# A kernel of attention and two feed-forward layers: elementwise work moved off GpSimd, plain products for 1,536 tokens, stored split weights, loads issued earlier

## Chip, cores, metric

One core of a Trainium2 chip. The metric is the device time of one execution in microseconds. The program is one kernel, written with an order of its own for every engine (no scheduler reorders it).

## What is computed

```python
scores = scale * np.matmul(q, k.transpose(0, 1, 3, 2))       # 4 x 8 heads, 576 tokens, 64
thresh = np.max(scores, axis=-1, keepdims=True) - tau
scores = np.where(scores >= thresh, scores, -1000000000.0)
attn = np.exp(scores - np.max(scores, axis=-1, keepdims=True))
attn = attn / (np.sum(attn, axis=-1, keepdims=True) + 1e-09)
x = np.matmul(attn, v)                                       # then 2304 tokens x 512
h = x @ w_in                                                 # layer one, 512 -> 2048
g = h * np.tanh(np.where(h > 20.0, h, np.log1p(np.exp(np.minimum(h, 20.0)))))
x = g @ w_out                                                # 2048 -> 512
y = ((x @ w_a) * (x @ w_b)) @ w_out2                         # layer two, 512 -> 1536 -> 512
```

q, k and v come as 32-bit floats, the weights as 64-bit floats.

## The kernel before

**Attention** runs in 80 units (16 pairs of heads, five units a pair), one per round of a loop. VectorE takes the scores from PSUM with their extreme (`least`) and masks the exponentials (`mask`), ScalarE forms the exponentials and copies transposed blocks out of PSUM, TensorE does scores, transposes and weighted sums. Results go to DRAM (`xd`).

**Conversion of weights.** `narrow` turns a 128-wide block of 64-bit weights into 32-bit ones by integer arithmetic on the two halves of each word, and writes it to DRAM (`wfd`). There are 68 such jobs. It is a generator: each `yield` is a place where it waits for its next turn. A job loads its raw block on SyncE's queue (`raw`), two turns later ScalarE and VectorE shift and mask it (lines 98 to 103), then GpSimd adds (107) and ScalarE squares (108), then VectorE masks small numbers to zero (110). In attention a job starts every `PACE` = 7 units; in the layers `narrow_some` gives each running job a turn per product.

**Layers.** Tokens are worked on in three superblocks of 768, each as two halves of 384. A step is a pair of 128-wide blocks of the hidden dimension: eight steps per superblock in layer one (h0 to h23), six in layer two (h24 to h41, each with products for w_a and for w_b). Every 32-bit operand is split into two parts (`hi` by ScalarE, the remainder by VectorE, line 155 for weights, 250 for x), and a product takes three matmuls for each of two 128-wide blocks. A step multiplies a 2 x 2 block matrix by seven products instead of eight: sums of blocks of the weights (`sums` in `in_weights`, tiles ws, GpSimd, line 181), sums of blocks of x (`sums` in `prepare`, GpSimd, 240), and combinations of the products afterwards (`after`: p1, p5 by ScalarE, u2, u3, c21, c12 by VectorE from PSUM, c22 by GpSimd, 342). Then the gate is applied (`gate` in layer one, the product of both branches in layer two), and `second` multiplies the result g by the out weights, one step later.

The place of a product is called a gap. `at_gap` hangs work into a later gap. Per gap the order of emission is: the product, what was hung there, a turn for conversions, some items of the weights of the next step (`feed`), the combination (`after`), the second products. Within an engine instructions run in this order. The weights' loads lead by two groups (one group is the weights of one kind for one step), in tiles `wf` with two buffers. The split weights of a step lie in one of three tiles (`wi_pools`). Products go to two PSUM tiles (`h`). `prepare` hangs the splits of x for a superblock into gaps from 6 before its start to 2 after it.

All loads and nearly all stores are issued from SyncE's queue, in order.

## Time and profile before

| | us |
|---|---|
| median of 3 runs | 1211.49 |
| lowest, highest | 1210.2, 1215.4 |
| the profiled execution | 1212.33 |
| its span, first to last instruction | 1210.5 |

| engine | busy us | share of the span |
|---|---|---|
| TensorE | 1116.2 | 92% |
| VectorE | 952.3 | 79% |
| ScalarE | 696.5 | 58% |
| GpSimd | 497.8 | 41% |

The engines are named PE, PEld (TensorE's weight loads), DVE (VectorE), ACT (ScalarE), POOL (GpSimd) and SP (SyncE). Matmuls are pipelined, so a busy TensorE is not one at its peak. An arrow names what was waited for. The share of busy time mixes stages with different limits: attention runs to about 295 us, layer one from there to 733, layer two to the end. The stretches below are cut at the first matmul of a step (h1 at 311.8, h8 at 447.7, h16 at 586.5, h24 at 733.5, h30 at 888.7, h36 at 1044.5).

### The profile page before, as it was taken

Reading aid. Unit: us, or ns where it says so; the run is one execution under the profiler, and the core shown is the slowest. Engines: PE = TensorE matmul, PEld = TensorE weight load, DVE = VectorE, ACT = ScalarE, POOL = GpSimd, SP = SyncE. Lnnn points to the kernel's source line nnn. Section 1 sums busy time; section 2 is a strip of 40 time slices with the busy share of each in tenths; the row PEclk is TensorE's granted clock in tenths of the full one; section 3 lists DMA queues with packets and bytes.
Section 4 is the critical chain, followed back from the end, with each engine's and each line's share of the span. In section 5 each row is a group of like instructions: output and inputs, shape, how many; then the busy total and the mean of one; then the engine's idle time right before and its main releaser. Section 6 shows DMA issues by size and latency. Waiting matters only on the chain.

```text
span 1210.5 us, 19202 instructions
## 1 busy us (share of the span) xinstructions
PE 1116.2 (92%) x6794; PEld 952.4 (79%) x6794; DVE 952.3 (79%) x1682; ACT 696.5 (58%) x1399; POOL 497.8 (41%) x502
## 2 busy tenths in 40 slices
...
GB/s 149 152 152 139 173 154 200 170 141 108 185 198 217 249 115 193 195 192 175 92 225 179 193 156 81 94 70 122 53 61 114 53 97 95 42 117 68 54 52 53
DMA packets 76993, 161.24 MB, mean 133 GB/s; under 512 B 6753, under 2 KB 36193, under 8 KB 76897
## 3 DMA queue, kind: packets, MB, share of 16 engines
...
q10 hardware_dynamic: 864, 1.08, 0.3%
...
## 4 chain that ended last, share of the span: by engine, by line
PE 60%; DVE 19%; issue 5%; DMA 5%; ACT 5%; POOL 4%; SPq 1%; DVEq 0%; POOLq 0%; ACTq 0%
PE acc L385 18%; PE tp L645 5%; PE sp L582 5%; PE sums_o L664 5%; DVE wii L155 2%; DVE wop L155 2%; DVE g L315 2%; DVE x L250 2%; DVE c21b L366 1%; POOL b L240 1%; DMA rawo<-w_out 1%; DVE s L590 1%; DVE woo L155 1%; DMA rawb<-w_b 1%; DVE pm L609 1%
## 5 line engine op out<-in xcount | busy, mean ns | idle before, releaser
L385 PE MATMUL acc<-g,woo 128*128 128x256 f32 (+1 forms) x1152 | 231.4, 344 | 0.0
L385 PEld LDWEIGHTS acc<-g,woo 128*128 128x128 f32 x1152 | 186.6, 194 | 17.4
L385 PE MATMUL acc<-g,wop 128*128 128x512 f32 (+1 forms) x864 | 172.2, 340 | 1.1 <-ACT g L320 0.7
L385 PEld LDWEIGHTS acc<-g,wop 128*128 128x128 f32 x864 | 139.0, 190 | 14.4 <-ACT g L320 0.9
L597 POOL TENSOR_TENSOR te<-m,bar 128x2 f32<-128x2 f32 (+1 forms) x80 | 44.8, 560 | 207.5 <-DVE s L590 207.5
L590 DVE TENSOR_SCALAR_CACHE_REDUCE s<-sp 128x576 f32<-128x576 f32 x144 | 103.4, 751 | 24.0 <-PE sp L582 20.4
L602 ACT ACTIVATE ex<-s,m 128x576 f32<-128x576 f32 x144 | 109.3, 771 | 16.1 <-DVE s L590 16.0
L646 ACT ACTIVATE pt<-tp 128x512 f32<-128x512 f32 (+1 forms) x192 | 90.8, 487 | 23.5 <-PE tp L645 21.6
L609 DVE SCALAR_TENSOR_TENSOR pm<-s,te,ex 128x576 f32<-128x576 f32 x128 | 100.7, 823 | 0.0
L645 PEld LDWEIGHTS tp<-ident,pm 128*128 128x128 f32 x576 | 63.4, 141 | 33.6 <-ACT ex L602 9.5
L645 PE MATMUL tp<-ident,pm 128*128 128x128 f32 x576 | 85.6, 280 | 4.5 <-ACT u L673 1.5
L315 DVE TENSOR_TENSOR g<-hs,g 128x384 fp32r<-128x384 f32 x96 | 84.8, 910 | 5.6 <-ACT g L314 5.4
L664 PE MATMUL sums_o<-pt,v 128*64 128x256 f32 x640 | 83.2, 390 | 0.0
L582 PE MATMUL sp<-k,qs 64*128 64x288 f32 x512 | 82.4, 429 | 0.8 <-DVE s L590 0.8
L342 POOL TENSOR_TENSOR c22a<-u3a,p5a 128x384 f32<-128x384 f32 x18 | 18.3, 1015 | 148.2 <-ACT p5a L340 148.2
L342 POOL TENSOR_TENSOR c22b<-u3b,p5b 128x384 f32<-128x384 f32 x18 | 19.7, 1094 | 125.0 <-DVE wop L155 91.8
L582 PEld LDWEIGHTS sp<-k,qs 64*128 64x128 f32 x512 | 46.5, 186 | 31.3 <-issue 8.6
L664 PEld LDWEIGHTS sums_o<-pt,v 128*64 128x64 f32 x640 | 40.3, 136 | 24.7 <-issue 7.1
L181 POOL TENSOR_TENSOR wsi<-wfi 128x256 f32<-128x256 f32 x48 | 50.0, 1041 | 19.4 <-DMA wfi<-wfi 19.4
L342 POOL TENSOR_TENSOR c22i<-u3i,p5i 128x384 f32<-128x384 f32 x24 | 29.2, 1219 | 55.0 <-ACT p5i L340 39.5
L155 DVE TENSOR_TENSOR wii<-wfi,wii 128x512 fp32r<-128x512 f32 (+1 forms) x48 | 45.4, 946 | 5.1 <-ACT wii L154 5.1
L155 DVE TENSOR_TENSOR woo<-wfo,woo 128x512 fp32r<-128x512 f32 x48 | 48.0, 1002 | 0.4
...
## 6 DMA issues: line engine op xcount, KB each, us to landing
...
```

Source lines behind the costliest of these rows:

```text
L155: lambda: V.tensor_tensor(out=dst()[1], in0=src(), in1=f32(dst()[0]), op=ALU.subtract),
L181: G.tensor_tensor(out=out, in0=x, in1=y, op=op)
L315: at_gap(gap + 1, lambda: V.tensor_tensor(out=gl, in0=hs, in1=f32(gh), op=ALU.subtract))
L342: G.tensor_tensor(out=o, in0=t["u3"], in1=t["p5"], op=ALU.add)
L385: PE.matmul(ps, w[:, a, f, c * 128:(c + 1) * 128], st.g[f][:, b, cols], start=st.first and f == 0 and m == 0 and (kind == "c" or c % 2 == ...
L582: PE.matmul(sp[:, half, 0:288], d["qs"][r, cols], d["k"][r, keys], start=True, stop=True)
L590: V.tensor_scalar(out=u["s"][:, h].rearrange("p (a c) -> p a c", a=2), in0=u["sp"][h][:, :, 0:288], scalar1=1.0, scalar2=None, op0=ALU.mul ...
L602: A.activation(u["e"][:, h], u["s"][:, h], AF.Exp, bias=u["m"][:, h:h + 1], scale=-1.0)
L609: V.scalar_tensor_tensor(out=u["pm"].rearrange("p a c -> p (a c)")[:, h * S:(h + 1) * S], in0=u["s"][:, h], scalar=u["te"][:, h:h + 1], in ...
L645: PE.transpose(tp[:, i], pm[:, j0 + i], ident)
L646: return lambda: A.activation(pt[:, j0:j0 + m], tp[:, :m], AF.Copy)
L664: PE.matmul(po[r], v[0][:, j + 4 * h, r], pair[pi][c & ~1][:, :, j + 4 * h], start=j == 0, stop=j == 4)
```

## The change

- The first two superblocks of layer one (`PLAIN`) are computed with eight plain products a step, two after one another into the same PSUM tile. Their weights are split as they are, without sums, x too (four splits instead of seven), and the gate reads PSUM directly.
- In the layers GpSimd gets no instruction any more: sums of weights and of x, c22 and the integer add of the conversion go to VectorE. In attention GpSimd keeps the add.
- A conversion has other instructions: one shift on VectorE instead of two masks, the mask for small numbers by a saturating copy on ScalarE and a clamp to -1 and 1 (by ScalarE in attention, by VectorE in the layers), then a product. The raw block is loaded four turns ahead instead of two. A job starts every 5 units in attention (16 jobs there instead of 12), and after that at rates of 0.45, 0.3, 0.3 per product and 0.25 in layer two.
- The split weights of w_a are stored in DRAM in the first superblock of layer two (from ScalarE's queue) and loaded as they are in the other two (1.8 MB a step, SyncE's queue).
- Loads of weights lead by three groups, in three buffers. A step of layer two has its w_a and out weights in its first seven gaps and w_b in the last seven.
- x of a superblock is made earlier, its sums in tiles of their own.

```diff
-T0, PACE = 1, 7
+T0, PACE = 1, 5
...
+PLAIN, PRE = {("i", 0), ("i", 1)}, {"i": 8, "a": 6}
+RATES = 0.45, 0.3, 0.3
...
-        yield A
-        yield A
-        u, a, o = tl("u", I32, 1), tl("a", I32, 2), tl("f", F32, 2)
-        A.activation(u, lo, AF.Copy, scale=2.0 ** -29)
-        V.tensor_scalar(
-            out=a, in0=hi.bitcast(I32), scalar1=3, scalar2=0x3FFFFFF8,
-            op0=ALU.logical_shift_left, op1=ALU.bitwise_and,
-        )
-        V.scalar_tensor_tensor(
-            out=a, in0=hi.bitcast(I32), scalar=-0x40000000, in1=a, op0=ALU.bitwise_and, op1=ALU.bitwise_or
+        for _ in range(4):
+            yield True
+        a, o = tl("a", I32, 2), tl("f", F32, 2)
+        A.activation(unit[:, 0::2].rearrange("p (c n) -> p c n", c=CC), lo, AF.Copy, scale=2.0 ** -29)
+        V.tensor_scalar(out=a, in0=hi.bitcast(I32), scalar1=3, scalar2=None, op0=ALU.logical_shift_left)
+        (G if acc_p is None else V).tensor_tensor(
+            out=a, in0=a, in1=unit.bitcast(I32).rearrange("p (c n) -> p c n", c=CC), op=ALU.add
...
-        yield G
-        G.tensor_tensor(out=a, in0=a, in1=u, op=ALU.add)
-        A.activation(o, hi.bitcast(F32), AF.Square)
-        yield V
-        V.scalar_tensor_tensor(out=o, in0=o, scalar=TINY, in1=a.bitcast(F32), op0=ALU.is_ge, op1=ALU.mult)
+        A.activation(o.bitcast(I32), hi.bitcast(F32), AF.Copy, scale=SEEN)
+        yield True
+        if acc_p is None:
+            A.activation(o, o.bitcast(I32), AF.Sign)
+        else:
+            V.tensor_scalar(out=o, in0=o.bitcast(I32), scalar1=-1.0, scalar2=1.0, op0=ALU.max, op1=ALU.min)
+        yield True
+        V.tensor_tensor(out=o, in0=a.bitcast(F32), in1=o, op=ALU.mult)
...
+    wpd = {
+        (kind, p): dram.tile([128, 2, 7, 256], F32, name=f"wp{kind}{p}") for kind, n in PRE.items() for p in range(n)
+    }
...
+        plain, first = (kind, s) in PLAIN, (kind, s - 1) in PLAIN or s == 0
+        kept = (kind, p) in wpd and not plain and not (first and s == NS - 1)
+
+        def tile_():
+            pool = wi_pools[count["wi"] % 3]
+            d["w"] = pool.tile([128, 2, 7, 256], F32R, tag="wi", name=f"wi{kind}{p}_{count['wi']}", bufs=1)
+            count["wi"] += 1
+
+        if kept and not first:
+
+            def fetch():
+                tile_()
+                nc.sync.dma_start(out=f32(d["w"]), in_=wpd[kind, p])
+
+            return None, [fetch], d
...
-            G.tensor_tensor(out=out, in0=x, in1=y, op=op)
+            V.tensor_tensor(out=out, in0=x, in1=y, op=op)
...
-        h0, l0 = part(0, 2, lambda: d["f"][:, 0].rearrange("p (k n) -> p k n", k=2))
+        def keep():
+            nc.scalar.dma_start(out=wpd[kind, p], in_=f32(d["w"]))
+
+        pair = lambda i: d["f"][:, i].rearrange("p (k n) -> p k n", k=2)
+        h0, l0 = part(0, 2, lambda: pair(0))
+        if plain:
+            h1, l1 = part(2, 4, lambda: pair(1))
+            return load, [start, h0, h1, l0, l1], d
...
-        ]
+        ] + [lambda: at_gap(now[0] + 2, keep)] * kept
...
-            if k == 1:
-                d["t"] = raw.tile([128, 2, NH], F32, tag="t", name=f"t_{layer}{s}", bufs=1)
-            out, x, y = (
-                (d[0, 0], d[0, 1], d[0, 0]), (d["t"] if k else None, d[1, 1], d[0, 0]),
-                (d[0, 1], d[1, 1], d[0, 1]), (d[1, 0], d[1, 0], d["t"] if k else None),
-            )[k]
-            for i in range(2):
-                G.tensor_tensor(out=out[:, i], in0=x[:, i], in1=y[:, i], op=ALU.subtract)
+            out, x, y = (("t1", "b01", "b00"), ("t2", "b11", "t1"), ("b01", "b11", "b01"), ("t4", "b10", "t2"))[k]
+            if out[0] == "t":
+                d[out] = raw.tile([128, 2, NH], F32, tag=out, name=f"{out}_{layer}{s}", bufs=1)
+            V.tensor_tensor(out=d[out], in0=d[x], in1=d[y], op=ALU.subtract)
...
-        return load, [
-            (1, H(0)), (2, L(0)), (2, T(0)), (3, H(2)), (3, T(1)), (4, L(2)), (4, H(1)), (4, T(2)), (5, L(1)),
-            (5, H(3)), (5, T(3)), (6, L(3)), (6, H(4)), (7, L(4)), (7, H(5)), (8, L(5)), (8, H(6)), (9, L(6)),
-        ]
+        if plain:
+            places = list(zip((-4, -3, -1, 0) if s else (0, 2, 4, 6), (0, 2, 3, 6)))
+        elif was:
+            places = list(zip((-8, -7, -6, -4, -3, -1, 0), (1, 4, 5, 0, 2, 3, 6)))
+        else:
+            places = [(k - 6, k) for k in range(7)]
+        items = [] if plain else [(k - 10, T(k)) for k in range(4)]
+        for at_, k in places:
+            items += [(at_, H(k)), (at_ + 1, L(k))]
+        return load, items
...
-                st.first, st.last, st.gaps = p == 0, p == pairs_ - 1, 7 * len(kinds)
+                st.first, st.last, st.plain = p == 0, p == pairs_ - 1, (kinds, s) in PLAIN
+                st.gaps = 8 if st.plain else 7 * len(kinds)
...
+    def plain_product(st, kind, n):
+
+        k, i, j = n // 4, n // 2 % 2, n % 2
+        w, x = st.w[kind]["w"], x_now[((0, 3), (2, 6))[j][k]]
+        if j == 0:
+            st.bank = h_p.tile([128, 512], F32, tag="h", name=f"h{st.i}{kind}{n}", bufs=2)[:, :NH]
+        for c in range(2):
+            for m, (a, b) in enumerate(((0, 0), (0, 1), (1, 0))):
+                PE.matmul(
+                    st.bank, w[:, a, 2 * i + j, c * 128:(c + 1) * 128], x[:, b, c], start=j == c == m == 0,
+                    stop=j == c == 1 and m == 2,
+                )
+
...
+        if st.plain:
+            if k % 2:
+                finish(st, kind, st.bank, k // 2 % 2, k // 4, gap)
+            return
...
-            G.tensor_tensor(out=o, in0=t["u3"], in1=t["p5"], op=ALU.add)
+            at_gap(gap + 1, lambda: V.tensor_tensor(out=o, in0=t["u3"], in1=t["p5"], op=ALU.add))
...
-        elif after_.gaps == 7:
-            places = [after_.base + 3 + k for k in range(6)]
+        elif after_.gaps < 14:
+            places = [after_.base + 3 - st.plain + k for k in range(6)]
...
-    groups.sort(key=lambda g: (g[0], g[1] == "out"))
+    groups.sort(key=lambda g: (g[0], 1 if g[1] == "out" else 2 * (g[2] == "b")))
...
-        n = sum(13 if what == "in" else 5 for j, what, _ in groups if j == i)
-        return [lambda: next(fed)] * n
+        n = [0, 0]
+        for k, g in enumerate(groups):
+            if g[0] == i:
+                n[g[2] == "b"] += len(loaded[k]) if k < len(loaded) else sizes(k)
+        return n
+
+    def spread(n, gaps):
+        return [n * (k + 1) // gaps - n * k // gaps for k in range(gaps)]
...
-        items = []
-
+        for _ in range(3):
+            load_group()
...
-            items = background(i)
+            early, late = background(i)
+            share = spread(early, st.gaps) if st.gaps < 14 else spread(early, 7) + spread(late, 7)
+            if i == 0:
+                share = [1] * 4 + spread(early - 4, 4)
+            elif st.gaps < 14 and late:
+                share = spread(early, 3) + spread(late, st.gaps - 3)
...
-                    at_gap(steps[i + 2].base - 7 + at_, fn)
+                    at_gap(max(steps[i + 2].base + at_, gap), fn)
...
-                        narrow_some(0 if st.last and not st.layer else 0.5 if i < 6 else 1 / 3)
-                    for _ in range(-(-len(items) // (st.gaps - (7 * j + k)))):
-                        items.pop(0)()
+                        narrow_some(0 if st.last and not st.layer else RATES[st.s] if not st.layer else 0.25)
+                    for _ in range(share[gap - st.base]):
+                        next(fed)
...
-        GROUPS = (0, 1, 1, 1, 1)
+        GROUPS = (0, 4, 1, 1)
...
-                if n == 52:
+                if n == 50:
...
```

VectorE in step h3, in the middle of the first superblock. Here wii and woo are the split weights, ai, fi, ao and fo the conversion's, u3, c21 and c12 the combinations, g the gate's remainder. Before:

```order
L110 SCALAR_TENSOR_TENSOR fi10_4376<-fi10_4376,ai10_4375 128x512
L99 TENSOR_SCALAR ai11_4424<-rawi11_4380 128x512
L103 SCALAR_TENSOR_TENSOR ai11_4424<-rawi11_4380,ai11_4424 128x512
L155 TENSOR_TENSOR wii4_4_4351<-wsi4_4_4352,wii4_4_4351 128x512 x2
L337 TENSOR_TENSOR u3i_3_4434<-h3i1_4364,p1i_3_4356 128x384
L110 SCALAR_TENSOR_TENSOR fi11_4425<-fi11_4425,ai11_4424 128x512
L99 TENSOR_SCALAR ao10_4455<-rawo10_4429 128x512
L103 SCALAR_TENSOR_TENSOR ao10_4455<-rawo10_4429,ao10_4455 128x512
L155 TENSOR_TENSOR woo3_10_4463<-wfo3_9_4327,woo3_10_4463 128x512
L346 TENSOR_TENSOR c21i_3_4485<-h3i1_4364,p1i_3_4356 128x384
L110 SCALAR_TENSOR_TENSOR fo10_4456<-fo10_4456,ao10_4455 128x512
L99 TENSOR_SCALAR ao11_4515<-rawo11_4460 128x512
```

Now:

```order
L365 TENSOR_TENSOR g0_3_4334<-hs00_3_4335,g0_3_4334 128x384
L116 TENSOR_TENSOR fo10_4320<-ao10_4319,fo10_4320 128x512
L164 TENSOR_TENSOR wii4_4_4325<-wfi4_8_4124,wii4_4_4325 128x512
L105 TENSOR_SCALAR ao11_4364<-rawo11_4293 128x512
L106 ISA ao11_4364<-ao11_4364,unit_153 128x1024
L164 TENSOR_TENSOR wii4_4_4325<-wfi4_8_4124,wii4_4_4325 128x512
L365 TENSOR_TENSOR g1_3_4371<-hs10_3_4372,g1_3_4371 128x384
L114 TENSOR_SCALAR fo11_4365<-fo11_4365 128x512
L116 TENSOR_TENSOR fo11_4365<-ao11_4364,fo11_4365 128x512
L365 TENSOR_TENSOR g0_3_4334<-hs01_3_4417,g0_3_4334 128x384
L105 TENSOR_SCALAR ai12_4434<-rawi12_4348 128x512
L106 ISA ai12_4434<-ai12_4434,unit_153 128x1024
```

The combinations and the sums are gone, the integer add (ISA, on 1,024 halves) stands among the conversion's instructions.

The end of step h26 in layer two, where the next step's second product needs the PSUM tile that c12b reads. VectorE, then GpSimd at the same place, before:

```order
L155 TENSOR_TENSOR wop2_60_8866<-wfp2_59_8760,wop2_60_8866 128x512
L346 TENSOR_TENSOR c21b_26_8886<-h26b1_8817,p1b_26_8803 128x384
L366 TENSOR_TENSOR c22b_26_8870<-c22b_26_8870,c22a_26_8764 128x384
L366 TENSOR_TENSOR c21b_26_8886<-c21b_26_8886,c21a_26_8776 128x384
L155 TENSOR_TENSOR wop2_60_8866<-wfp2_59_8760,wop2_60_8866 128x512
L350 TENSOR_TENSOR c12b_26_8899<-h26b4_8856,u2b_26_8826 128x384
L366 TENSOR_TENSOR c12b_26_8899<-c12b_26_8899,c12a_26_8792 128x384
```

```order
L342 TENSOR_TENSOR c22b_26_8870<-u3b_26_8854,p5b_26_8868 128x384
L181 TENSOR_TENSOR wsa4_32_8919<-wfa4_60_8864 128x256
L181 TENSOR_TENSOR wsa4_32_8919<-wsa4_32_8919,wfa4_60_8864 128x256
L181 TENSOR_TENSOR wsa4_32_8919<-wfa4_60_8864 128x256
L181 TENSOR_TENSOR wsa4_32_8919<-wfa4_60_8864,wsa4_32_8919 128x256
```

VectorE now (GpSimd has no instruction here):

```order
L396 TENSOR_TENSOR c22b_26_8528<-u3b_26_8514,p5b_26_8526 128x384
L164 TENSOR_TENSOR wib3_31_8460<-wsb3_32_8461,wib3_31_8460 128x512
L400 TENSOR_TENSOR c21b_26_8544<-h26b1_8477,p1b_26_8463 128x384
L420 TENSOR_TENSOR c22b_26_8528<-c22b_26_8528,c22a_26_8419 128x384
L420 TENSOR_TENSOR c21b_26_8544<-c21b_26_8544,c21a_26_8432 128x384
L164 TENSOR_TENSOR wib3_31_8460<-wsb3_32_8461,wib3_31_8460 128x512
L404 TENSOR_TENSOR c12b_26_8557<-h26b4_8516,u2b_26_8486 128x384
L420 TENSOR_TENSOR c12b_26_8557<-c12b_26_8557,c12a_26_8451 128x384
```

c22b's add came to VectorE ahead of c21b. Between c21b and c12b stand a product for c22b, one for c21b and one split, as before.

VectorE in h23, the last step of layer one, where x and the weights of layer two are made (x0 to x6 are the splits of x, t and t1 to t4 its sums). Before:

```order
L332 TENSOR_TENSOR u2i_23_8053<-h23i1_8032,p1i_23_8024 128x384
L250 TENSOR_TENSOR x0_10_8039<-b00_10_7819,x0_10_8039 128x768
L155 TENSOR_TENSOR wia0_24_8017<-wsa0_24_8018,wia0_24_8017 128x512
L315 TENSOR_TENSOR g0_23_8086<-hs00_23_8087,g0_23_8086 128x384
L110 SCALAR_TENSOR_TENSOR fp11_8044<-fp11_8044,ap11_8043 128x512
L155 TENSOR_TENSOR wib0_25_8082<-wfb0_49_7993,wib0_25_8082 128x512
L337 TENSOR_TENSOR u3i_23_8108<-h23i1_8032,p1i_23_8024 128x384
L250 TENSOR_TENSOR x2_10_8096<-b10_10_7823,x2_10_8096 128x768
L155 TENSOR_TENSOR wib0_25_8082<-wfb0_49_7993,wib0_25_8082 128x256
L155 TENSOR_TENSOR wib0_25_8082<-wsb0_25_8083,wib0_25_8082 128x512
L250 TENSOR_TENSOR x1_10_8124<-t_10_8098,x1_10_8124 128x768
L155 TENSOR_TENSOR wib0_25_8082<-wsb0_25_8083,wib0_25_8082 128x512
```

Now:

```order
L204 TENSOR_TENSOR wsb0_26_7722<-wfb0_50_7610 128x256
L204 TENSOR_TENSOR wsb0_26_7722<-wsb0_26_7722,wfb0_50_7610 128x256
L391 TENSOR_TENSOR u3i_23_7726<-h23i1_7651,p1i_23_7643 128x384
L278 TENSOR_TENSOR x2_10_7712<-b10_10_7442,x2_10_7712 128x768
L114 TENSOR_SCALAR fa11_7716<-fa11_7716 128x512
L164 TENSOR_TENSOR wib0_25_7721<-wfb0_50_7610,wib0_25_7721 128x512
L204 TENSOR_TENSOR wsb0_26_7722<-wfb0_50_7610 128x256
L278 TENSOR_TENSOR x3_10_7742<-b01_10_7440,x3_10_7742 128x768
L396 TENSOR_TENSOR c22i_23_7751<-u3i_23_7726,p5i_23_7749 128x384
L116 TENSOR_TENSOR fa11_7716<-aa11_7715,fa11_7716 128x512
L164 TENSOR_TENSOR wib0_25_7721<-wfb0_50_7610,wib0_25_7721 128x256
L204 TENSOR_TENSOR wsb0_26_7722<-wfb0_50_7610,wsb0_26_7722 128x256
```

The sums of w_b (wsb) and c22 came in between the splits of x; the conversion of w_a's last block (aa11, fa11) stands there too.

## Rows read from the trace of the kernel before

**Rows 1.** Busy time by stretch: PE, PEld, DVE, ACT, POOL, PEclk, DMA share, GB/s

```profile
294.60:311.80 17.20, 12.84 (x73) 11.22 (x73) 8.78 (x14) 8.62 (x19) 5.87 (x6) 0.80 0.50 171
311.80:447.70 135.90, 115.56 (x613) 103.71 (x612) 125.17 (x172) 81.14 (x162) 79.82 (x64) 0.95 0.60 195
447.70:586.50 138.80, 129.75 (x721) 119.17 (x720) 125.59 (x168) 86.87 (x176) 78.88 (x65) 0.98 0.52 175
586.50:733.50 147.00, 134.50 (x722) 122.08 (x720) 129.47 (x174) 89.87 (x183) 83.46 (x71) 0.95 0.51 172
733.50:888.70 155.20, 142.89 (x804) 133.18 (x804) 101.35 (x162) 66.45 (x133) 62.90 (x69) 1.00 0.24 84
888.70:1044.50 155.80, 143.74 (x793) 134.46 (x793) 101.93 (x164) 64.94 (x129) 62.78 (x69) 0.97 0.24 82
1044.50:1210.50 166.00, 151.59 (x846) 141.19 (x846) 97.41 (x164) 60.52 (x123) 46.92 (x54) 0.98 0.20 67
483.60:499.30 15.70, 15.70 (x91) 14.66 (x90) 14.57 (x21) 9.95 (x20) 9.99 (x9) 1.00 0.61 207
811.40:835.80 24.40, 23.33 (x135) 21.96 (x134) 15.19 (x27) 9.37 (x20) 8.35 (x11) 1.00 0.19 65
888.70:918.40 29.70, 26.60 (x133) 25.04 (x134) 21.83 (x32) 13.89 (x28) 12.76 (x14) 0.83 0.28 98
```

**Rows 2.** TensorE's waits, 300 to 740 us: total, times, longest us

```profile
PE h3i L291 <- DVE u2i L332: 2.7, 1, 2.7
```

**Rows 3.** TensorE's waits, 740 to 1,212 us

```profile
PE h27a L291 <- DVE c12b L350: 1.1, 1, 1.1
```

**Rows 4.** Timeline of a step's end in layer two: start us, us, instruction

```profile
810.55 1.06 POOL L181 TENSOR_TENSOR wsa<-wfa 128x256 f32<-128x256 f32 x1
...
810.93 1.09 DVE L366 TENSOR_TENSOR c21b<-c21b,c21a 128x384 f32<-128x384 f32 x1
...
811.95 1.22 DVE L155 TENSOR_TENSOR wop<-wfp,wop 128x512 fp32r<-128x512 f32 x1
...
813.09 0.55 DVE L350 TENSOR_TENSOR c12b<-h26b,u2b 128x384 f32<-128x384 f32 x1
...
813.69 1.34 PE L291 MATMUL h27a<-x,wia 128*128 128x384 f32 x6 [1.07 <-DVE c12b L350]
```

**Rows 5.** VectorE, groups by shape, 745 to 870 us: busy, mean ns

```profile
L155 DVE TENSOR_TENSOR wia<-wsa,wia 128x512 fp32r<-128x512 f32 x11 | 7.5, 682 | 0.0
...
L155 DVE TENSOR_TENSOR wia<-wfa,wia 128x256 fp32r<-128x256 f32 x5 | 2.1, 419 | 0.0
```

**Rows 6.** ScalarE's waits, 300 to 740 us

```profile
ACT ui L98 <- DMA rawi<-w_in: 14.3, 7, 3.4
...
ACT uo L98 <- DMA rawo<-w_out: 13.0, 6, 4.1
```

**Rows 7.** The chain that ended last, in order of time: start us, us, what

```profile
73.33 1.45 PE sums_o L664 x12
...
90.17 1.45 PE sums_o L664 x12
...
231.56 1.45 PE sums_o L664 x12
...
252.26 1.45 PE sums_o L664 x12
...
335.31 4.09 DMA rawi<-w_in
...
488.68 2.09 PE h10i L291 x12
```

**Rows 8.** VectorE, groups by shape, 311 to 450 us

```profile
L99 DVE TENSOR_SCALAR aa<-rawa 128x512 int32<-128x512 int32 x2 | 0.9, 427 | 1.1 <-DMA rawa<-w_a 1.1
```

**Rows 9.** ScalarE, groups by shape, 0 to 300 us

```profile
L98 ACT ACTIVATE ui<-rawi 128x512 int32<-128x512 uint32 x6 | 4.1, 689 | 0.0
```

**Rows 10.** VectorE, groups by shape, 460 to 740 us

```profile
L315 DVE TENSOR_TENSOR g<-hs,g 128x384 fp32r<-128x384 f32 x62 | 52.2, 869 | 5.2 <-ACT g L314 5.0
```

47 lines of the change are left out of this document (28 added, 19 removed).

## Prediction, made before the changed kernel was run

> **What bounds the kernel now.** I read the busy time by stretches first, then who made TensorE wait, then one stretch of the timeline, then single durations. In the windows the reader should hold TensorE's time against a step at its floor. A step of layer one is 90 matmuls, and where nothing disturbs them they take 15.7 us with TensorE busy throughout (the stretch from 483.6 to 499.3 us) [rows 1]. The first 1,536 tokens run well above that: seven steps (h1 to h7) in 135.9 us, 19.4 each, with VectorE busy for 125.17 of it. The third superblock needs 147.0 for eight steps. There TensorE waits for VectorE's u2, u3 and c12, as at h3 [rows 2]. Layer two runs at 24.4 us a step, and a step beside a change of superblock takes 29.7 at a granted clock of 0.83, that is partly at the lower of the two levels, 1.2 and 2.4 GHz (from 888.7 to 918.4) [rows 1].
>
> In layer two each step loses 1.1 us to one wait, for c12 of the second product [rows 3]. The timeline shows its origin [rows 4]: three VectorE instructions stand in a row. The product of c21 takes 1.09 us and the split of wop 1.22 us while GpSimd forms sums; c12 behind them takes 0.55. The same shape as the split takes 0.682 elsewhere, and 384 elements take 0.55 [rows 4, 5]. So GpSimd's work stretches VectorE instructions that read two SBUF tensors, and they stand in TensorE's way. ScalarE's second loss is for raw weights: 13 waits of 2.1 us on w_in and w_out alone [rows 6].
>
> So the bound is TensorE's own work in 5 of 8 steps of the middle superblock, VectorE stretched by GpSimd in the first, and queues at the changes of superblock.
>
> **The change, part by part**, against the profiled execution: span 1210.5, time 1212.33, 0.07% above the median of 1211.49.
>
> *Plain products.* A step has eight products of six matmuls instead of seven: six more, at 2.09 us for twelve [rows 7], are 1.04 us. Sixteen steps: +16.7 us, all on TensorE. A plain step's floor is 16.74. In exchange VectorE loses u2, u3, c21, c12 and half of the weight splits, and GpSimd everything. From the listing, VectorE's step h3 has now 7 two-tensor instructions of 512 (0.682 each [rows 5]), 4 of 384 (0.55), 6 one-source ones (0.427 [rows 8]) and 3 integer adds: 4.8 + 2.2 + 2.6 + 2.0 = 11.6 us, so it hides behind TensorE.
>
> *The integer add on VectorE.* No row shows it. It handles 512 words as 1,024 halves. Bounds: the row of 512 elements, 0.682, and 1,024 elements by the slope between 256 and 512 (0.419 and 0.682, so 1.03 ns an element), 1.21. I take 0.68, the row with the same bytes. The higher price would leave h3 at 13.2, still hidden. The Trainium skill (VectorE: DVE Perf Modes, section "Specifications") says that integers are converted and exact only below 2^24, so the built-in add wouldn't do; its section "The perf-mode tier table (the rule you actually need)" gives two-tensor instructions on 16-bit data twice the fp32 rate. By that rule the add is about 0.69 (my estimate from the page) and the sum stays; by one element per cycle it would be 1.21 and the sum some 7 us more. No run here shows it yet.
>
> *Sums and c22 on VectorE.* In the third superblock a step (h20) has 7 of 512, 9 of 384, 5 of 256, 4 one-source and 2 adds: 4.8 + 5.0 + 2.1 + 1.7 + 1.4 = 14.9, against 15.7 of TensorE: just hidden. In h23 to h25 it isn't. There the x of layer two, the sums of both w_a and w_b and the last conversions meet: h23 has 11 of 512, 9 of 384, 6 of 768 (0.946 by the same slope), 10 of 256, 3 one-source, 2 adds, 24.9 us; h24 and h25 count to 24.1 and 24.6. TensorE's floor is 15.7, 25 and 23.4. VectorE becomes the bound for these three steps: 73.6.
>
> *GpSimd idle.* c21, wop's or wib's split and c12 still follow one another at a step's end (the listing has the same four rows), but unstretched: (1.09 - 0.55) + (1.22 - 0.68) = 1.08 us earlier, which is the 1.07 that TensorE waits [rows 4]. So 24.4 becomes 23.4. VectorE's load is 19.5 in the first superblock of layer two, 15.4 in the others, so cover remains. c22 on VectorE stands a product earlier, where VectorE idles.
>
> *Stored split weights.* 48 fewer splits on ScalarE and VectorE each, nearly all hidden. Cost: six stores on ScalarE's queue and twelve loads of 1.8 MB. At the pace of 512 KB in 4.09 us [rows 7] one takes 14.3, issued a step (23.4) ahead: hidden. Two loads queue behind it, with a lead of a step themselves.
>
> *Loads ahead.* A raw load is used four products after its issue: 4 x 2.09 = 8.4 us, before 2 x 2.8 (19.4 / 7) = 5.6. The 2.8 us exceed the mean wait of 2.1. Most waits go; I leave 2 us per superblock.
>
> *x made earlier, sums in own tiles.* At a change of superblock no GpSimd chain stands ahead of TensorE; VectorE's h29 counts 23.9 against 23.4. Next late is VectorE, by about a microsecond.
>
> *Attention.* A group of five units takes 16.84 us (73.33 to 90.17) where no conversion runs, 20.70 where x and weights are prepared [rows 7]. Conversions rise from 12 to 16, VectorE's share of one falls by 0.7 (one instruction fewer), ScalarE's grows by one of 0.69 [rows 9]; three of seven x splits and two of four weight splits go. Bounds -10 and +16 (below); I take -2. The hand-over (from 294.6 to 311.8) [rows 1] gains 3 (ScalarE's u no longer queues behind a weight load) and pays 1 for more matmuls.
>
> **The sum** by the windows of [rows 1]:
>
> - to 311.8: -4
> - h1 to h7: 7 x 16.74 + 2 = 119.2 for 135.9: -16.7
> - h8 to h15: 8 x 16.74 + 2 = 135.9 for 138.8: -2.9
> - h16 to h23: 7 x 15.7 + 3 + 24.9 = 137.8 for 147.0: -9.2
> - h24 to h29: 48.7 + 3 x 23.4 + 24.3 = 143.2 for 155.2: -12.0
> - h30 to h35: 24.9 + 4 x 23.4 + 24.3 = 142.8 for 155.8: -13.0
> - rest: 4 for its first step, 1 for each of four, 0.5 at the end: -8.5
>
> Together -66.3: span 1144.2, time 1146.
>
> **Rivals.**
>
> *Loads still late.* SyncE issues a raw load behind the write of an older job, which waits for VectorE, so the lead may be eaten. If each of 52 conversions in the layers still costs ScalarE 1 us and half reaches TensorE, +26: 1172. For: the queue's order hasn't changed. Against: a load alone takes 4.09 us [rows 7].
>
> *The integer add is dear.* Two adds a step at +0.53: h16 to h22 go to 15.2 to 16.9, +4; h23 to h25 +3.2: 1153.
>
> *ScalarE in attention.* 16 jobs of three instructions instead of 12 of two, at 0.69: +16 us, all on the path: 1162. For: ScalarE and VectorE alternate there. Against: 12 conversions cost little over 16.84 a group.
>
> *The stored weights don't hide.* If a load takes twice 14.3 beside the others, TensorE waits 5.2 us twelve times, +62: 1208, no change. Against: a window of layer one moves 207 GB/s at a DMA share of 0.61, layer two would need 124.
>
> *Slower: the stretch isn't GpSimd's.* If g's 0.869 [rows 10] against 0.55 comes from another source (ScalarE, DMA), VectorE gets GpSimd's work at the stretched price, 1.58-fold on all that doesn't read PSUM. Then h16 to h22 need 22.3 a step (+46), h23 to h25 109 (+36), h1 to h7 19.9 (+20), h26 to h29 28 or more (+23): 1271. It turns slower at about 1.3-fold. Against it: in one and the same step the shape of 512 takes 0.682 with GpSimd idle and 1.22 with it busy [rows 4, 5]. The Trainium skill (GPSIMD Engine Reference, section "Key points") names contention with VectorE instructions that have two SBUF inputs, which the trace bears out: 1.09 against 0.55.
>
> **Chances and range.** Forecast (1125 to 1160) 0.62, loads late 0.14, dear add 0.08, ScalarE 0.06, slower 0.05, stored weights 0.03, better than 1125 0.02. Low 1122: no pile-up in h23 to h25 (-10), attention at -10, 6 less of the residues. High 1182: late loads (+26), the dear add (+7), 3 us more at changes of superblock. Faster by over 0.5% (about the least that a measurement of this kernel tells from no change) 0.92, within it 0.03, slower 0.05.
>
> **What would show it.** VectorE's splits of 512 at 0.69 all over the layers, g at 0.55; steps h9 to h14 16.7 apart, h26 to h28 23.4 with no wait on c12; ScalarE's waits on raw weights under 15 us in all; a pile-up of 8 to 10 us at h23 to h25. Wrong, if 384-element instructions stay near 0.87 with GpSimd idle, if an attention group of five goes beyond 18, or if TensorE waits on wia.

## The result: 1211.42 to 1130.72 us, and the profile after

The changed kernel takes 1130.72 us (median of 4 runs, 1129.95 to 1132.05), the kernel before 1211.42 beside it: a ratio of 0.933, 95% interval 0.9307 to 0.9353. That is inside the range of the prediction (1122 to 1182) and 15 us below its forecast of 1146. The profiled execution has a span of 1130.3 us, against 1210.5.

TensorE is now busy for 98% of the span, VectorE for 73%, GpSimd for 6%. The first section of its page:

```profile
PE 1102.8 (98%) x6890; PEld 955.1 (85%) x6890; DVE 827.0 (73%) x1757; ACT 647.6 (57%) x1297; POOL 67.6 (6%) x102
```

The windows of the changed kernel, cut at the first matmul of h1, h8, h16, h23, h24, h25, h26, h30, h31, h36, answer to [rows 1]. The columns are the same: TensorE, its weight loads, VectorE, ScalarE, GpSimd, then granted clock, DMA share and GB/s.

```profile
304.00:421.40 117.40, 117.40 (x674) 109.91 (x674) 78.87 (x147) 67.76 (x132) 0.00 (x0) 1.00 0.69 228
421.40:555.40 134.00, 134.00 (x769) 125.55 (x769) 76.34 (x138) 70.80 (x142) 0.00 (x0) 1.00 0.49 166
555.40:664.40 109.00, 107.53 (x614) 100.09 (x613) 87.12 (x178) 69.16 (x143) 0.00 (x0) 1.00 0.54 181
664.40:685.30 20.90, 17.57 (x91) 15.91 (x90) 20.60 (x40) 14.15 (x27) 0.00 (x0) 0.92 0.52 195
685.30:711.80 26.50, 25.48 (x146) 23.80 (x145) 22.26 (x46) 15.47 (x32) 0.00 (x0) 1.00 0.65 228
711.80:737.80 26.00, 23.60 (x135) 21.88 (x134) 22.32 (x48) 12.75 (x27) 0.00 (x0) 1.00 0.64 233
737.80:832.00 94.20, 93.55 (x531) 87.43 (x529) 71.71 (x143) 40.54 (x78) 0.00 (x0) 1.00 0.42 151
832.00:858.50 26.50, 24.95 (x133) 23.57 (x134) 17.35 (x34) 11.07 (x24) 0.00 (x0) 0.94 0.39 142
858.50:974.30 115.80, 115.78 (x662) 109.40 (x660) 75.39 (x147) 42.49 (x83) 0.00 (x0) 1.00 0.40 145
974.30:1130.30 156.00, 149.15 (x846) 139.59 (x846) 88.87 (x175) 49.70 (x102) 0.00 (x0) 1.00 0.30 110
```

In the first two superblocks of layer one TensorE's busy time equals the window: no wait is left there, so only fewer or shorter matmuls could make it shorter. The loss stands in the rows from 664.4 to 737.8 (h23 to h25), at h30 and h36, and in the last step (from 1092.7 us on TensorE is busy for 32.9 of 37.6).

Set against the forecast, by the prediction's own windows (us; before, forecast and measured change):

| stretch | before | after | forecast | measured |
|---|---|---|---|---|
| to h1 | 311.8 | 304.0 | -4 | -7.8 |
| h1 to h7 | 135.9 | 117.4 | -16.7 | -18.5 |
| h8 to h15 | 138.8 | 134.0 | -2.9 | -4.8 |
| h16 to h23 | 147.0 | 129.9 | -9.2 | -17.1 |
| h24 to h29 | 155.2 | 146.7 | -12.0 | -8.5 |
| h30 to h35 | 155.8 | 142.3 | -13.0 | -13.5 |
| rest | 166.0 | 156.0 | -8.5 | -10.0 |
| sum | 1210.5 | 1130.3 | -66.3 | -80.2 |

TensorE's waits in the changed kernel from 280 us on, the longest ones (total us, times, longest). c12b, for which nearly every step of layer two waited 1.1 us [rows 3], is left only at h25, h30 and h36; h26 to h28 wait 0.2 for u2a, and for the inner steps of the last two superblocks no wait is listed.

```profile
PE h23i L341 <- DVE u2i L386: 3.3, 1, 3.3
...
PE h36a L341 <- DVE c12b L404: 1.6, 1, 1.6
PE h30a L341 <- DVE c12b L404: 1.6, 1, 1.6
...
PE h25a L341 <- DVE u2a L386: 1.4, 1, 1.4
PE h25a L341 <- DVE c12b L404: 1.0, 1, 1.0
...
PE h26a L341 <- DVE u2a L386: 0.2, 1, 0.2
```

VectorE's groups by shape over the whole run (busy, mean ns of one): the integer add (the page calls it CUSTOM_DVE), the split of the out weights, g. The last two answer to [rows 5] and [rows 10].

```profile
L365 DVE TENSOR_TENSOR g<-hs,g 128x384 fp32r<-128x384 f32 x96 | 52.7, 556 | 94.4 <-ACT g L364 94.4
L164 DVE TENSOR_TENSOR woo<-wfo,woo 128x512 fp32r<-128x512 f32 x48 | 31.5, 685 | 0.0
...
L106 DVE CUSTOM_DVE_ANT_0 ap<-ap,unit 128x1024 uint16<-128x1024 uint16 x12 | 8.3, 693 | 4.0 <-ACT unit L104 2.8
```

The add takes 693 ns (forecast 0.68 us), the split 685 everywhere, g 556 where it took 869 on average in the kernel before. For the add the trace thus agrees with the Trainium skill (VectorE: DVE Perf Modes, section "The perf-mode tier table (the rule you actually need)"), which gives a two-tensor instruction on 16-bit data twice the rate; the upper bound of 1.21 is out.

### The profile page after: what moved, and what is told of

It is laid out like the page before. It is cut to its first block, busy times and chain, and to the rows that moved or that the text cites. A ratio compares the mean times of both kernels' runs of the same rounds, so it can differ in the third digit from the quotient of the medians.

```text
span 1130.3 us, 18718 instructions
## 1 busy us (share of the span) xinstructions
PE 1102.8 (98%) x6890; PEld 955.1 (85%) x6890; DVE 827.0 (73%) x1757; ACT 647.6 (57%) x1297; POOL 67.6 (6%) x102
## 4 chain that ended last, share of the span: by engine, by line
PE 86%; DVE 8%; ACT 3%; issue 1%; DMA 1%; SPq 0%; POOL 0%; DVEq 0%; POOLq 0%; ACTq 0%
PE acc L439 29%; PE sums_o L734 6%; PE sp L652 6%; PE tp L715 6%; PE sp L654 1%; DVE x L278 1%; ACT ex L672 1%; PE sums_o L738 1%; PE warm L619 1%; PE h5i L322 1%; PE h12i L322 1%; PE h7i L322 1%; PE h15i L322 1%; PE h3i L322 1%; PE h14i L322 1%
## 5 line engine op out<-in xcount | busy, mean ns | idle before, releaser
L439 PE MATMUL acc<-g,woo 128*128 128x256 f32 (+1 forms) x1152 | 226.5, 339 | 0.0
L439 PEld LDWEIGHTS acc<-g,woo 128*128 128x128 f32 x1152 | 182.1, 189 | 16.9
L365 DVE TENSOR_TENSOR g<-hs,g 128x384 fp32r<-128x384 f32 x96 | 52.7, 556 | 94.4 <-ACT g L364 94.4
L660 DVE TENSOR_SCALAR_CACHE_REDUCE s<-sp 128x576 f32<-128x576 f32 x144 | 103.8, 754 | 18.7 <-PE sp L652 14.1
L679 DVE SCALAR_TENSOR_TENSOR pm<-s,te,ex 128x576 f32<-128x576 f32 x128 | 115.5, 939 | 0.0
L459 ACT ACTIVATE ys<-acc 128x512 f32<-128x512 f32 (+1 forms) x44 | 20.7, 488 | 33.1 <-PE acc L439 33.1
L370 ACT ACTIVATE g<-s 128x384 fp32r<-128x384 f32 x18 | 9.5, 527 | 44.2 <-DVE s L420 44.2
L164 DVE TENSOR_TENSOR woo<-wfo,woo 128x512 fp32r<-128x512 f32 x48 | 31.5, 685 | 0.0
L370 ACT ACTIVATE g<-c22b 128x384 fp32r<-128x384 f32 x18 | 9.5, 526 | 38.3 <-DVE c22b L420 38.3
L164 DVE TENSOR_TENSOR wii<-wfi,wii 128x512 fp32r<-128x512 f32 (+1 forms) x48 | 30.2, 641 | 0.0
L163 ACT ACTIVATE wii<-wfi 128x512 fp32r<-128x512 f32 (+1 forms) x48 | 28.5, 595 | 2.7 <-DMA wfi<-wfi 2.7
```

The source lines that it names most:

```text
L164: lambda: V.tensor_tensor(out=dst()[1], in0=src(), in1=f32(dst()[0]), op=ALU.subtract),
L365: at_gap(gap + 1, lambda: V.tensor_tensor(out=gl, in0=hs, in1=f32(gh), op=ALU.subtract))
L439: PE.matmul(ps, w[:, a, f, c * 128:(c + 1) * 128], st.g[f][:, b, cols], start=st.first and f == 0 and m == 0 and (kind == "c" or c % 2 == ...
L660: V.tensor_scalar(out=u["s"][:, h].rearrange("p (a c) -> p a c", a=2), in0=u["sp"][h][:, :, 0:288], scalar1=1.0, scalar2=None, op0=ALU.mul ...
L679: V.scalar_tensor_tensor(out=u["pm"].rearrange("p a c -> p (a c)")[:, h * S:(h + 1) * S], in0=u["s"][:, h], scalar=u["te"][:, h:h + 1], in ...
```

## Experiments

The kernel before was timed beside every run on the same chip, and ratios to it are compared. The column "us" is the difference of ratios times 1211. Each edit is shown against the base that the table names (that of e11 against the changed kernel); "..." marks lines left out.

| run | base | edit | ratio to before (95%) | us against its base |
|---|---|---|---|---|
| the change | before | all | 0.933 (0.9307 to 0.9353) | -81 |
| e1_sums_gpsimd | after | sums, c22 on GpSimd | 0.939 (0.9372 to 0.9408) | +7 |
| e2_plain_first_only | after | second superblock not plain | 0.9293 (0.9278 to 0.9308) | -4.5 |
| e3_no_store | after | no stored weights | 0.9401 (0.9387 to 0.9415) | +8.6 |
| e4_lead2 | after | raw lead two | 0.9719 (0.969 to 0.9747) | +47 |
| e13_lead3 | after | raw lead three | 0.9378 (0.936 to 0.9397) | +5.8 |
| e9_int_gpsimd | after | integer add on GpSimd | 0.9319 (0.9305 to 0.9333) | -1.3 |
| e5_before_lead4 | before | raw lead four | 0.991 (0.9894 to 0.9927) | -11 |
| e10_before_vector_sums | before | sums, c22 on VectorE | 0.9897 (0.9882 to 0.9912) | -12.5 |
| e12_before_lead4_sums | before | both | 0.9726 (0.9706 to 0.9746) | -33 |
| e7_rates_plain | e2 | conversions earlier | 0.9248 (0.923 to 0.9265) | -5.4 |
| e11_no_plain | e7 | first superblock not plain either | 0.9384 (0.936 to 0.9408) | +16.5 |
| e14_rate55 | e7 | still denser conversions | 0.9247 (0.9233 to 0.9261) | -0.1 |

### Is it GpSimd's work that stretches VectorE? e1 and e10

```diff
-            V.tensor_tensor(out=out, in0=x, in1=y, op=op)                # in_weights, sums
+            G.tensor_tensor(out=out, in0=x, in1=y, op=op)
-            at_gap(gap + 1, lambda: V.tensor_tensor(out=o, in0=t["u3"], in1=t["p5"], op=ALU.add))
+            at_gap(gap + 1, lambda: G.tensor_tensor(out=o, in0=t["u3"], in1=t["p5"], op=ALU.add))
```

> The changed kernel, with the sums of the weights and c22 back on GpSimd in the layers (the integer add and the sums of x stay on VectorE). Theory A, GpSimd's work stretches VectorE's instructions with two SBUF operands: the split of 512 elements goes from 0.685 to between 0.8 and 1.2 us, and c12b makes TensorE wait about 1 us in most steps of layer two again; +15 us (10 to 22), 1141 to 1153. Theory B, the stretch of the kernel before had another source: the durations stay at 0.685, VectorE only has less to do, and the time is 1127 to 1132.

Measured: +7 us. The durations follow theory A, the time only in part. Timeline of e1 around the start of h27 (start, duration, instruction):

```profile
768.00 0.55 DVE L420 TENSOR_TENSOR c21b<-c21b,c21a 128x384 f32<-128x384 f32 x1
...
769.23 0.74 POOL L204 TENSOR_TENSOR wsa<-wfa 128x256 f32<-128x256 f32 x1 [2.96 <-DVE wib L164]
...
770.31 1.09 DVE L371 TENSOR_TENSOR g<-c22b,g 128x384 fp32r<-128x384 f32 x1
```

An instruction of 384 elements with both operands in SBUF takes 0.55 before GpSimd starts and 1.09 beside it. (The 0.55 of c12b that the prediction set against the 1.09 reads one operand from PSUM, so it was not the like case.) So the stretch is GpSimd's; the rival that ended slower than before falls. But the loss is confined to the first superblock of layer two (154.1 us for 146.7), in which GpSimd forms sums of w_a at a step's start: three steps (h26 to h28) take 74.2 us there, 24.7 each for 23.6, and h31 to h35 take 115.7, as in the changed kernel (115.8). The wait that comes back is for u2a (1.3 us in each of h26 to h28, 0.2 in the changed kernel), not for c12b as theory A had it.

```profile
743.90:818.10 74.20, 70.27 (x398) 65.61 (x397) 47.74 (x79) 27.79 (x59) 28.20 (x30) 1.00 0.42 153
866.90:982.60 115.70, 115.70 (x663) 109.55 (x662) 64.58 (x117) 42.27 (x84) 26.19 (x30) 1.00 0.40 145
```

In the last two superblocks the split w_a comes from DRAM, so no sum of w_a runs where c12b and u2a stand. The other direction, on the kernel before:

```diff
-            G.tensor_tensor(out=out, in0=x, in1=y, op=op)                # in_weights, sums
+            V.tensor_tensor(out=out, in0=x, in1=y, op=op)
-                G.tensor_tensor(out=out[:, i], in0=x[:, i], in1=y[:, i], op=ALU.subtract)
+                V.tensor_tensor(out=out[:, i], in0=x[:, i], in1=y[:, i], op=ALU.subtract)
-            G.tensor_tensor(out=o, in0=t["u3"], in1=t["p5"], op=ALU.add)
+            at_gap(gap + 1, lambda: V.tensor_tensor(out=o, in0=t["u3"], in1=t["p5"], op=ALU.add))
```

> The kernel before, with the sums of the weights, the sums of x and c22 on VectorE instead of GpSimd; the integer add of the conversion stays on GpSimd. Theory A, the stretch comes from GpSimd's work: layer two loses about 1 us a step (18 us), layer one 5 to 12, together 18 to 30 us less. Theory B, the stretch has another source and VectorE gets 2.2 us a step more at stretched prices: 15 to 40 us more.

Measured: -12.5 us, less than theory A's 18 to 30. In the profiled executions layer two gives 11.8 (465.2 us for 477.0), the second and third superblock of layer one 6.3, and 3.2 are lost before h1. The same place as in [rows 4], in this run:

```profile
805.42 0.55 DVE L366 TENSOR_TENSOR c21b<-c21b,c21a 128x384 f32<-128x384 f32 x1
805.89 0.69 DVE L155 TENSOR_TENSOR wop<-wfp,wop 128x512 fp32r<-128x512 f32 x1
```

The same two instructions took 1.09 and 1.22 beside GpSimd, so the durations are theory A's. One step there, and what TensorE waits for at the start of the next:

```profile
781.90:806.00 24.10, 23.46 (x134) 21.90 (x133) 17.40 (x37) 9.43 (x20) 0.00 (x0) 1.00 0.20 66
```

```profile
PE h27a L291 <- DVE u2a L332: 0.6, 1, 0.6
```

c12b is on time, and a step falls from 24.4 to 24.1, not to 23.4: the sums of w_a, now on VectorE, stand ahead of u2a, for which TensorE waits 0.6. An idle GpSimd with its sums on VectorE, in the order of the kernel before, gives 0.3 us in an inner step; the forecast put the whole 1.08 down to it. The steps at a change of superblock gain more (h30 takes 27.5 for 29.7). The first superblock of layer one gains nothing (136.0 for 135.9).

### Do the stored weights matter? e3

```diff
-PLAIN, PRE = {("i", 0), ("i", 1)}, {"i": 8, "a": 6}
+PLAIN, PRE = {("i", 0), ("i", 1)}, {}
```

> The changed kernel without stored split weights: w_a is split anew in each superblock of layer two. Theory A, VectorE and ScalarE have cover there (15.1 of 23.2 us a step busy, with about 4 more on VectorE): 1130 to 1133, no difference. Theory B, the splits stand ahead of c12 and u2 and TensorE waits 0.5 to 1 us in each of twelve steps: 1137 to 1143.

Measured: +8.6 us, theory B. VectorE's order at the start of h32 in this run:

```profile
885.65 0.42 DVE L204 TENSOR_TENSOR wsa<-wfa 128x256 f32<-128x256 f32 x1
...
886.93 0.42 DVE L204 TENSOR_TENSOR wsa<-wsa,wfa 128x256 f32<-128x256 f32 x1
887.26 0.68 DVE L164 TENSOR_TENSOR wia<-wfa,wia 128x512 fp32r<-128x512 f32 x1
887.86 0.55 DVE L386 TENSOR_TENSOR u2a<-h32a,p1a 128x384 f32<-128x384 f32 x1
```

Two sums and a split of w_a (885.65, 886.93, 887.26) stand ahead of u2a; without them it would come some 1.3 us earlier. A step takes 118.3 / 5 = 23.7 us instead of 115.8 / 5 = 23.2, and h30 28.6 instead of 26.5, although VectorE is busy for 92.2 of 118.3 only:

```profile
831.90:860.50 28.60, 25.22 (x132) 23.21 (x133) 20.77 (x42) 12.92 (x28) 0.00 (x0) 0.94 0.27 92
860.50:978.80 118.30, 117.32 (x663) 109.35 (x661) 92.22 (x187) 52.03 (x104) 0.00 (x0) 1.00 0.26 86
```

TensorE's listed wait for u2a is 0.2 us a step; the rest is not listed as a wait but stands in its busy time, which for the same products is 0.3 us a step longer (117.32 for 115.78 in five steps). That the half microsecond comes with the splits of w_a is shown; that their place ahead of u2a is the reason is read from the order alone. The prediction called these splits "nearly all hidden": by their sum they would have been.

### The lead of raw loads: e4, e13, e5

```diff
-        for _ in range(4):
+        for _ in range(2):
             yield True
...
-        GROUPS = (0, 4, 1, 1)
+        GROUPS = (0, 2, 1, 1)
```

> The changed kernel with the raw block of a conversion loaded two products ahead in the layers (two units ahead in attention as before, so attention is unchanged). Theory A, ScalarE waits for raw data again, but TensorE stands far enough behind: +0 to +5, 1131 to 1136. Theory B, each late load holds up ScalarE's queue and half of it reaches TensorE, as priced in the prediction: +15 to +26, 1146 to 1157.

Measured: +47 us, more than either theory allowed. ScalarE's waits for raw blocks are 123.3 us from 280 to 700 us (54.8 in layer one of the kernel before, from 300 to 740 us, and 26.1 in that of the changed one, from 290 to 700). The three longest rows:

```profile
ACT unit L104 <- DMA rawp<-w_out: 39.3, 8, 12.9
ACT unit L104 <- DMA rawb<-w_b: 36.5, 10, 6.7
ACT unit L104 <- DMA rawa<-w_a: 29.7, 8, 6.1
```

One cycle of it, timeline in h11 (SPq is SyncE's queue: an issue; in brackets the idle time before and its cause):

```profile
480.99 0.79 ACT L104 ACTIVATE unit<-rawb 128x512 int16<-128x512 uint32 x1 [4.89 <-DMA rawb<-w_b]
...
483.08 1.32 PE L322 MATMUL h11i<-x,wii 128*128 128x384 f32 x6 [1.47 <-ACT g L364]
...
485.13 0.32 SPq L117 DMA_DIRECT2D wfb<-fb  x1
...
485.50 0.43 SPq L98 DMA_DIRECT2D rawp<-w_out  x1
...
490.43 0.79 ACT L104 ACTIVATE unit<-rawp 128x512 int16<-128x512 uint32 x1 [6.12 <-DMA rawp<-w_out]
```

ScalarE stands 4.89 us for rawb; the gate behind it is late, the PSUM tile of a plain product comes free late, and TensorE stands 1.47. Then SyncE issues the load of the next raw block at 485.50, right behind the write of an older job (485.13) that had waited for VectorE, which had waited for ScalarE. The block is usable at 490.43, 4.9 us later, and ScalarE has waited again, 6.12 us. So a delay puts off the next load; that the cycle repeats itself is read from this timeline and not tested. The prediction had this queue as a rival, at +26; with a lead of two it would have been right in kind and too small. In a plain step the gate reads PSUM directly, so ScalarE's queue stands in TensorE's way there: h8 to h15 take 151.9 for 134.0. The steps with seven products lose as well, h16 to h25 take 209.0 for 182.4. From h26 on, with the last conversion's add begun at 779 us, e4 takes the same 392.5 us as the changed kernel.

```diff
-        for _ in range(4):
+        for _ in range(3):
...
-        GROUPS = (0, 4, 1, 1)
+        GROUPS = (0, 3, 1, 1)
```

> The changed kernel with a raw block loaded three products ahead, 6.3 us. With two products (4.2 us) it was 47 us slower than with four. Theory A, a load that is queued behind an older job's write needs its 4.1 us and some 3 us of queue: ScalarE still waits, +5 to +20. Theory B, only the bare load of 4.1 us has to be covered: within 4 us of the changed kernel.

Measured: +5.8 us, theory A at its lower end. It is lost at two places, in h1 to h7 (122.6 for 117.4, with one wait of 7.7 us for rawb in h6) and in h24 (29.6 for 26.5, with one of 4.6). From two to four products the cost goes 47, 5.8, 0: no even slope, as one would expect if delays at a lead of two feed the next ones.

On the kernel before, the lead alone:

```diff
-        yield A
-        yield A
+        for _ in range(4):
+            yield A
...
-        GROUPS = (0, 1, 1, 1, 1)
+        GROUPS = (0, 2, 2, 1, 1)
```

> The kernel before, with one edit: a raw block is loaded four products ahead of its use instead of two (in attention as before). Theory A, late raw data holds up ScalarE there as it does in the changed kernel with a lead of two, where 123 us of ScalarE's waits cost TensorE 47: of the 55 us of waits in the layers most go, and a half reaches TensorE: 8 to 25 us less. Theory B, products of 2.8 us give a lead of two enough cover and VectorE, stretched by GpSimd, sets the pace: within 4 us of the kernel before.

Measured: -11 us, theory A. ScalarE's raw waits in layer one go from 54.8 to 3.9 us, but 21.9 us of waits for GpSimd's integer add take their place, in the first superblock. The gain stands in the third superblock (136.1 for 147.0) and a little in the second; in the first, where VectorE is busy for 131.9 of 136.3 us, there is none.

### Do the two add up? e12

The edits of e5 and e10 together.

> The kernel before with both edits, raw loads four products ahead and the sums of weights, of x and c22 on VectorE. Alone they gave 11 and 12 us. Theory A, they act at different places (ScalarE's raw data in layer one, c12 in layer two) and add up: 20 to 25 us less, 1186 to 1191. Theory B, both shorten the same waits: 12 to 17 us less, 1194 to 1199.

Measured: -33 us, where the two alone gave 23.5: both theories fall. Layer two gains what it gained in e10 (465.1); the second and third superblock of layer one now gain 8.5 and 14.1 against 2.7 and 10.9 with the lead alone, and 2.2 and 4.1 with the sums alone. So the second superblock gains more than the two alone (8.5 for 4.9), the third a little less (14.1 for 15.0), and the first gains 1.8 where each alone gave nothing; h1 begins 6.3 us later than before (3.2 with the sums alone). By these stretches of the profiled executions the surplus is some 2 us, by the ratios 10. That in the second superblock ScalarE's data and VectorE's combinations were late in the same steps, so that mending one alone gave little, would explain its part; it is not shown.

### Plain products, and where the conversions stand: e2, e7, e11, e14

```diff
-PLAIN, PRE = {("i", 0), ("i", 1)}, {"i": 8, "a": 6}
+PLAIN, PRE = {("i", 0)}, {"a": 6}
```

> The changed kernel, with only the first superblock of layer one in plain products; the second is computed with seven products a step. Theory A, TensorE is the bound there and VectorE (76 of 134 us busy now) has room for u2, u3, c21, c12, c22, the sums and three splits more: the eight steps go from 134.0 to 125 to 127 us, the whole to 1121 to 1125. Theory B, VectorE's place in the order and not its load decides: waits for u2 and u3 come back as in the kernel before, and the time is 1130 to 1140.

Measured: -4.5 us against the changed kernel. On the scale of 1211 that is 1126 us, a microsecond above theory A (1128.45 beside 1214.35 on that chip). The eight steps take 126.4, as theory A had it. Steps h10 to h14 take 15.7 to 15.8 us, TensorE's floor with seven products, with VectorE carrying the combinations; some 3 us go at h9, h15 and h16, and h24 to h29 take 2.5 more (149.2): with fewer products in layer one the last conversion falls later among the steps (its add begins 2.4 us ahead of h26, in the changed kernel 14.0). So the second superblock pays six matmuls a step for cover that it doesn't need.

e7 has the edit of e2, and besides:

```diff
-RATES = 0.45, 0.3, 0.3
+RATES = 0.45, 0.45, 0.45
```

> The changed kernel with only the first superblock of layer one in plain products, and with 0.45 conversions started per product in all of layer one instead of 0.45, 0.3, 0.3. Theory A, the last six conversions (about 2.2 us of VectorE each) add to the pile-up of h23 to h25 and go out of it: 3 to 6 us less than with plain products in the first superblock only. Theory B, the same conversions make the second superblock, computed with seven products, wait for VectorE: no gain, up to 5 us more.

Measured: 0.9248, 5.4 us less than e2 and 9.9 us (0.9%) less than the changed kernel. The last conversion's add begins at 652.7 us instead of 723.8. Windows of h23, h24 and h25:

```profile
660.30:678.00 17.70, 16.02 (x91) 14.63 (x90) 17.54 (x34) 13.31 (x26) 0.00 (x0) 1.00 0.63 224
678.00:703.90 25.90, 25.39 (x145) 23.72 (x144) 19.10 (x39) 13.38 (x29) 0.00 (x0) 1.00 0.49 181
703.90:727.50 23.60, 23.44 (x134) 21.88 (x133) 17.31 (x37) 9.89 (x22) 0.00 (x0) 1.00 0.48 178
```

They take 67.2 us (73.4 in the changed kernel, 73.4 in e2: 19.7, 27.6, 26.1). So conversions were in TensorE's way in h23 to h25. At h25 TensorE had waited for u2a and c12b, and in the changed kernel's order a shift and an add of a conversion (begun at 715.73 and 716.29 us) stand ahead of h25's u2a (717.83), a product of one (712.19) ahead of c12b (713.39). VectorE's load had been 22.3 of 26.0 us there, below the window, which points again to their place and not their sum; no run moved them within the step.

```diff
-PLAIN, PRE = {("i", 0), ("i", 1)}, {"i": 8, "a": 6}
+PLAIN, PRE = set(), {"a": 6}
...
-RATES = 0.45, 0.3, 0.3
+RATES = 0.45, 0.45, 0.45
...
-                    plan(55, [(2 * k, item) for k, item in rest])
+                    plan(52, [(2 * (k + 10), item) for k, item in rest])
```

The lines left out make room for the sums of the first weights and of x in attention.

> The changed kernel with seven products a step in all of layer one (no plain products) and 0.45 conversions started per product there; x and the first weights of layer one get their sums in attention as well. Theory A, without GpSimd's stretch VectorE carries the combinations in the first superblock too (11.3 of 16.8 us a step busy now): h1 to h7 take 108 to 112 us instead of 117.4, the whole is 4 to 9 us shorter than with plain products in the first superblock alone, 1111 to 1117. Theory B, VectorE is the bound in the first superblock, as in the kernel before, and plain products are worth their matmuls there: 1120 to 1135.

Measured: 16.5 us more than e7, theory B. The first superblock, h1 to h7:

```profile
307.70:437.30 129.60, 115.24 (x613) 103.39 (x614) 113.53 (x228) 83.68 (x165) 0.00 (x0) 0.96 0.60 195
```

```profile
PE h3i L344 <- DVE c12i L407: 2.2, 1, 2.2
PE h5i L344 <- ACT p1i L386: 2.0, 1, 2.0
PE h1i L344 <- DVE c12i L407: 2.0, 1, 2.0
```

129.6 us for 117.3. VectorE isn't full (113.5), and TensorE waits for one thing after another, c12 and ScalarE's p1 most. h1 begins 3 us later as well (307.7 for 304.6), as the first sums are formed in attention. In the first superblock, with a conversion begun every third product, plain products are worth their matmuls; of the prediction's exchange, +16.7 on TensorE was needed for eight steps, not sixteen.

```diff
-RATES = 0.45, 0.45, 0.45
+RATES = 0.55, 0.45, 0.45
```

> The changed kernel with plain products in the first superblock of layer one only, and 0.55, 0.45, 0.45 conversions started per product in the three superblocks. With 0.45 throughout two conversions still stood in h15 (4.5 us of VectorE's 19.0 there) and the ratio to the kernel before was 0.9248. Theory A, VectorE has room in the first superblock (79 of 117 us busy), the conversions leave h15, and it gains 2 to 4 us: ratio 0.921 to 0.923. Theory B, denser conversions wait for each other's writes on SyncE's queue and raw data come late in the first superblock: 2 to 10 us lost, ratio 0.926 to 0.933.

Measured: 0.9247, no change against e7; neither theory. The last add begins at 620 instead of 653 us, but h15 still has two of them and takes 19.3 us as before; what was gained in the third superblock (127.3 for 129.0) was lost at h8 (17.0 for 14.3). The forecast took the rates at face value, by which in e14 all 52 conversions would have been begun before h15. In the code the credit for conversions is capped at one, so 0.45 begins one every third product, 0.55 every second, 0.3 and 0.25 every fourth, and some are left for h15.

### The integer add: e9

```diff
-        (G if acc_p is None else V).tensor_tensor(
+        G.tensor_tensor(
```

> The changed kernel with the integer add of the conversion on GpSimd in the layers too, nothing else on it there. Theory A, it takes GpSimd 1.5 us and stretches VectorE's neighbours by half a microsecond each, 52 times in all, while VectorE is spared 0.69: TensorE mostly has cover, +2 to +8 against the changed kernel. Theory B, VectorE is short of time in h23 to h25 and is relieved: -1 to -4.

Measured: -1.3 us, within the interval of no difference; theory A's cost isn't there. GpSimd's adds do stretch a neighbour, the clamp of a conversion (L114). Timeline, GpSimd's adds and the clamps:

```profile
321.17 1.29 POOL L106 TENSOR_TENSOR ao<-ao,unit 128x512 int32<-128x512 int32 x1 [3.86 <-DVE ao L105]
...
323.51 0.42 DVE L114 TENSOR_SCALAR fo<-fo 128x512 f32<-128x512 int32 x1
...
327.55 1.30 POOL L106 TENSOR_TENSOR ai<-ai,unit 128x512 int32<-128x512 int32 x1 [5.09 <-DVE ai L105]
...
327.72 1.42 DVE L114 TENSOR_SCALAR fi<-fi 128x512 f32<-128x512 int32 x1 [0.31 <-ACT fi L109]
```

The clamp takes 0.42 us after GpSimd is done and 1.42 beside it; over all 52 its mean is between 0.82 and 1.10 by tile, 0.42 in the changed kernel. What VectorE is spared (0.69 an add) and what it pays are about equal: it is busy for 828.1 us in all, 827.0 in the changed kernel. So of "GpSimd idle in the layers" the sums and c22 matter, not the add.

## Why the prediction was right, and where its steps were not

**The sign and most of the size.** Its floors hold: plain steps are 134.0 / 8 = 16.75 (16.74 forecast), the inner steps of layer two 23.1 to 23.6 (23.4), the add 0.693 (0.68), the pile-up in h23 to h25 is 73.4 us (73.6).

**The pile-up's 73.6 came out by luck.** The sum for h23 was made from the right instructions: the window from 664.4 has 40 instructions where the listing gave 41, one split of 512 elements fewer and otherwise shape for shape. But it took 20.9 us, not 24.9, with VectorE busy for 20.6 of it. The step that failed is adding durations. VectorE in h23 (timeline: start, duration, instruction):

```profile
670.11 0.55 DVE L365 TENSOR_TENSOR g<-hs,g 128x384 fp32r<-128x384 f32 x1
670.58 0.68 DVE L116 TENSOR_TENSOR fa<-aa,fa 128x512 f32<-128x512 f32 x1
671.18 0.42 DVE L164 TENSOR_TENSOR wia<-wfa,wia 128x256 fp32r<-128x256 f32 x1
671.52 0.42 DVE L204 TENSOR_TENSOR wsa<-wfa,wsa 128x256 f32<-128x256 f32 x1
```

An instruction of 0.55 is followed after 0.47, one of 0.68 after 0.60, one of 0.42 after 0.34: back to back, each begins 0.08 us before the one ahead ends. Over 40 instructions that is some 3 of the 4.0 us, and the missing split is another 0.6. [rows 4] showed it already (810.93 + 1.09 is past 811.95). The Trainium skill (Perfetto Trace Analysis, section "Optimizing Scalar/DVE Operations") gives such an instruction a fixed overhead for data access of about 60 ns in SBUF and says that its profiled latency is about twice that, as the half in which the write is acknowledged overlaps with the next instruction. The trace agrees that there is an overlap; here it is 80 ns. In h24 and h25 it went the other way: 52.5 for 48.7. Conversions are the reason for most of it (with them gone from there, 53.7 in e2 became 49.5 in e7).

**Residues, attention.** h16 to h22, forecast at 7 x 15.7 + 3, took 109.0, 15.6 each; the 2 or 3 us left for residues in each superblock of layer one weren't needed. Of the 14 us by which the forecast was too slow, these are 7.6 (1.8, 1.9 and 3.9), the time to h1 is 3.8 (attention gained 3.2 us and the hand-over 4.6, for 2 and 2), layer two outside h24 and h25 2.3. h23's 4.0 were given back at h24 and h25. No run took attention and the hand-over alone. The traces show where attention's 3.2 us stand: its first nine groups of five units after the start take 16.84 us each (from 20.34 to 171.90), though a conversion now begins in every one; before it was 16.84 to 18.96 (from 19.79 to 177.83). That is 6.5 us gained; from there to h0, where x and weights are prepared, it takes 2.7 us longer. So the rival of ScalarE in attention (+16) isn't there. Neither is the one of stored weights that don't hide: h31 to h35 take 23.1 to 23.3 us each, and no wait of TensorE for the load of wia is listed.

**Layer two: right in sum, wrong in causes.** 32.0 us gained, 33.5 forecast. The forecast gave it to idle GpSimd (e10: 12 us with GpSimd's sums on VectorE and the old order), nothing to stored weights (e3: 8.6 us when taken away). Between e12's layer two (465.1) and e3's (454.4) lie another 11 us that no run took apart: w_b's items in a step's last seven gaps, weights loaded three groups ahead, x made earlier, its sums in own tiles.

**Layer one: the lead was worth more than "most waits go".** ScalarE's raw waits in layer one went from 54.8 to 26.1 us, not to under 15. They stand in h1 to h15, where TensorE's busy time equals the window, so it lost none of it. In the changed kernel a lead of two instead of four costs 47 us (e4), in the kernel before it cost 11 (e5). The price of the rival "loads still late", 26, was an average share of a wait, and the waits of e4 exceeded it; if delays feed the next ones, as its timeline suggests, no fixed share would have priced them.

Of the 80 us, with parts measured on different bases, so no strict sum: the lead and the sums on VectorE 33 (e12), plain products in the first superblock some 16 (e11 against e7), stored weights 8.6 (e3). Plain products in the second superblock take 4.5 back (e2). The remainder, near 27, is the time to h1 (304.0 for e12's 318.1, 14 us; 311.8 before) and the order in layer two (11). No run took these two apart, nor the conversion's new instructions, so their causes stay open.

## The better version

e7, with plain products in the first superblock alone and all conversions begun every third product in layer one, takes 1120.74 us (1117.68 to 1121.12): 0.9248 of the kernel before, and 0.9% below the changed kernel (intervals 0.923 to 0.9265 and 0.9307 to 0.9353).
